# One pool for all eight PSUM banks, with a planner that follows each bank

## The chip, the cores and the metric

The kernel runs on one core of one Trainium2 chip. A core has five engines that run side by side, each through its own list of instructions: TensorE (PE in the profile) multiplies matrices, VectorE (DVE) and ScalarE (ACT) work elementwise and read TensorE's results, GpSimd (POOL) works elementwise on data in SBUF alone here, and SyncE (SP) issues nearly all transfers. TensorE writes its results into PSUM, which has eight banks. A bank holds 128 partitions x 512 float32 values, the largest result of one product here. Semaphores order the engines: an instruction that reuses a bank waits until the last reader of the bank has finished.

The metric is the time of one execution on the device in microseconds (us), as the median of several runs.

## The reference

Two parts follow each other. First comes attention by way of 32 learned points ("inducing"), for 4 batches of 12480 tokens with 128 channels:

```python
def mab(q, kv):
    s = scale * (q @ kv.transpose(0, 2, 1))
    s = s - s.max(-1, keepdims=True)
    a = np.exp(s)
    a /= a.sum(-1, keepdims=True) + 1e-09
    return a @ kv
h = mab(I, x)           # 32 points look at all tokens
return mab(x, h)        # all tokens look at the 32 results
```

Then comes a layer with a leaky relu, on all 49920 tokens, with 2048 hidden channels:

```python
h = x @ w_in
g = np.maximum(h, 0.0) + alpha * np.minimum(h, 0.0)
return g @ w_out
```

## The kernel before, in words

Tokens are taken in tiles of 128, and sixteen tiles make a superblock: six full ones per batch and a short rest. A token's attention output is a mixture of only 32 rows, so the first product of the layer is made from the 32 weights of each token: for each batch the kernel forms HW, the 32 results times w_in, and multiplies by the tokens' weights, which stand transposed in the tile `a` (a2 in the code). The leaky relu is split. The relu part goes through ACT or DVE, and then through a second product with W1, which is w_out scaled by one minus alpha. The linear part is one small product with a matrix HA per batch.

The main work is a chain of *visits*. A block is four tiles (512 tokens), and a block is visited four times, since each visit makes four of the sixteen groups of 128 hidden channels. In one visit TensorE makes four products into four banks (`visit`, L761). Each is read by one relu, on ACT (L774) or DVE (L776), which writes a tile `gt`. Behind these four products TensorE makes sixteen products from the `gt` tiles of the visit *before* (`second`, L787), which add up in the block's sum bank. At the first visit of every second block, `linear` (L814) adds the linear part into the sums of two blocks, and takes the second block's bank if it has none. When a block is complete, `finish` copies the sum to SBUF on ACT (L840) or DVE (L842; four early blocks at L833) and SP stores it (L847).

Between visits small pieces of work for the next superblock or batch are placed. For the next superblock: the scores (L597), their copy to SBUF (L655 on ACT, L657 on DVE), the maximum (L674, DVE), a subtraction (L679, GpSimd), the exponential (L641, ACT), a tree of sums (L665, GpSimd), a reciprocal (L702, DVE), the normalised weights in four copies (`rep`, L710, GpSimd) and a transposing transfer into `a` (L719, SP). For the next batch: loading x (L275), a cast (L290, GpSimd), a transposing transfer (`xT`, L313), scores (L336) and their reduction (L350, DVE), an exponential (L375, ACT), another transposing transfer (`e`, L406) and the sum over tokens (L430) with its addition (L446, DVE). SP works through loads, transposing transfers and stores in the order in which they were written down.

Two things fix the order. Which visit a small piece follows is written out by hand: `at(n, ...)` puts it behind visit n, with a list of its costs by engine. Which engine takes each relu and each copy, and whether a piece of elementwise work is done at once or late (between the second and third relu of the next visit, `run_waiting`), is chosen by the class `Plan` when the kernel is built: a search that keeps 64 states and steps through all visits with a small model of the engines' times. In that model a product of visit n has to wait for a relu that is fixed by a ring of six banks, and one number stands for when the separate bank is free.

The banks before: a pool of six, `hhps`, goes round for the four products of each visit and for everything in the opening. A second pool has two banks, bp0 and bp1. The blocks' sums alternate between them; after visit 8 a small product goes into the one that the current block doesn't use (`spare`).

Before the visits comes the opening (`order`, a list of steps by hand), in which the first batch's attention is made with casts and transposes on several engines and some empty products on TensorE ("W6") in between. One bank, `later`, keeps the scores of most of the first superblock until visit 1.

Of the kernel before, what the change touches and what calls it, by code (L numbers as in the profile page):

```python
# [21 lines left out]
P = 128  # L22
R = 4
ST = 16
# [6 lines left out]
def kernel(  # L31
# [55 lines left out]
    H = ST // 2  # L87
# [18 lines left out]

    hh_ps = ctx.enter_context(tc.tile_pool(name="hhps", bufs=6, space=bass.MemoryType.PSUM))
    b_ps = ctx.enter_context(tc.tile_pool(name="bps", bufs=1, space=bass.MemoryType.PSUM))

    ctx.enter_context(tc.manual_schedule())  # L110

    class Plan:
# [6 lines left out]
        FREE, MODE, SEM, ARRIVE = 56, 98, 62, 233  # L119
        WIDTH = 64  # L120

        def __init__(self):

            self.visits = []
            self.taken = None
            self.waiting = []

        def on_act(self):
# [14 lines left out]
        def step(self, state, n, relus, ways):  # L143


            pe, a, v, e1, e2, late, bank = state
            cols, last, linear, chains = self.visits[n]
            busy = {"a": a, "v": v}
            need = (e2[2], e2[3], e1[0], e1[1])
            hh = []  # L150
            for r in range(R):
                pe = max(pe, need[r] + self.SEM) + 4
                hh.append(pe + cols * 0.417 + self.ARRIVE)
            out = []
            for r in range(R):
                if r == 2:
                    for k, ns, ready, reads in late:
                        busy[k] = max(busy[k], ready) + ns
                        bank = busy[k] + 100 if reads else bank
                lat, per, over = self.RELU[relus[r]]  # L160
                out.append(max(busy[relus[r]], hh[r]) + lat + per * cols)
                busy[relus[r]] = out[r] - over
            pe += cols * 0.417
            if linear:
                pe = max(pe, bank + self.SEM) + linear
            pe += self.MODE
            for r in range(R):
                pe = max(pe, e1[r] + self.SEM) + last * self.FREE
            waits = []
            for chain, way in zip(chains, ways):  # L170
                ready, reads = 0, False
                for kind, ns in chain:
                    if kind == "!":
                        continue
                    if kind in "ps":
                        pe = max(pe, bank + self.SEM) if kind == "s" else pe
                        pe += ns
                        ready, reads = pe + self.ARRIVE, True
                        continue
                    k = way[0] if kind == "f" else kind  # L180
                    ns = self.COPY[k] if kind == "f" else ns
                    if way[-1:] == "l":
                        waits.append((k, ns, ready, reads))
                    else:
                        busy[k] = ready = max(busy[k], ready) + ns
                        bank = ready + 100 if reads else bank
                    reads = False
            return pe + self.MODE, busy["a"], busy["v"], tuple(out), e1, tuple(waits), bank

        def choose(self):  # L190
            zero = (0.0,) * R
            beam = [((0.0, 0.0, 0.0, zero, zero, (), 0.0), None)]
            relus = ["".join(w) for w in product("av", repeat=R) if 0 < w.count("a") < R]
            for n, (_, _, _, chains) in enumerate(self.visits):
                ways = []
                for chain in chains:
                    kinds = [k for k, _ in chain]
                    when = ["n", "l"] if len(ways) + 1 == len(chains) or "s" not in kinds else ["n"]
                    if "f" in kinds:
                        ways.append([e + w for e in "av" for w in when])  # L200
                    elif "!" in kinds or not {"a", "v"} & set(kinds):
                        ways.append([""])
                    else:
                        ways.append(when)
                found = {}
                for state, path in beam:
                    for way in product(*ways):
                        for relu in relus:
                            new = self.step(state, n, relu, way)
                            at = new[0] + 390  # L210
                            over = max(new[1] - at, 0) + max(new[2] - at, 0)
                            over += sum(w[1] for w in new[5]) * 0.3
                            score = new[0] + 0.3 * over
                            key = (*(int(x - new[0]) // 16 for x in new[1:3] + new[3]), new[5])
                            if key not in found or score < found[key][0]:
                                found[key] = (score, new, (path, relu + "".join(way)))
                best = sorted(found.values(), key=lambda f: f[0])[: self.WIDTH]
                beam = [(new, path) for _, new, path in best]
            path, taken = beam[0][1], []
            while path:  # L220
                path, these = path
                taken.append(these)
            self.taken = iter("".join(reversed(taken)))

    plan = Plan()

    def ring(shape, dtype=f32):
        return hh_ps.tile(shape, dtype, name="hh", tag="hh")

    def sums(k):  # L230

        return b_ps.tile([P, 512], f32, name="bp", tag=f"bp{k % 2}")

    spare = None

    def small(shape):

        if spare is None:
            return ring(shape)
        return b_ps.tile(shape, f32, name="hh", tag=f"bp{spare % 2}")  # L240

# [316 lines left out]
    def a_w_copy(st, act=True):  # L558
# [7 lines left out]
        plan.then(work)  # L566

    def a_lin(st):
# [210 lines left out]
    def second(blk, i, gts):  # L779
        nt = blk.nt  # L780
        if blk.acc is None:
            blk.acc = sums(blk.k)
        for r, gt in enumerate(gts):
# [15 lines left out]
    def linear(pair):  # L799


        for blk in pair:
            if blk.acc is None:
                blk.acc = sums(blk.k)
        products = [
# [106 lines left out]
    def warm(n):  # L912

        ps = sums(0)
        for _ in range(n):
            nc.tensor.matmul(ps[:, : 2 * P], blank[:, :P], blank[:], start=True, stop=True)  # L916
# [38 lines left out]
    w0 = rep0[:, :, 0, :]  # L955
    later = b_ps.tile([P, ST, M], f32, name="bp", tag="bp1")

# [197 lines left out]
    at(1, first_rest_less, H, H, cost=[("v", 780), ("!", 0)])  # L1155
    at(2, first_turn, cost=[("p", 350), ("f", 0)])
# [3 lines left out]
    at(6, linear_product, cost=[("p", 900), ("v", 210), ("!", 0)])  # L1160
    at(7, a_lin, st, cost=[("p", 260), ("v", 210)])
    blocks[0].later = True

# [23 lines left out]
    for b in range(B - 1):  # L1187
# [29 lines left out]
    for n, (blk, i) in enumerate(visits):  # L1217
        nt = visits[n - 1][0].nt * visits[n - 1][0].per if n else 0
        chains = [cost for _, _, cost in todo.get(n, ()) if cost]
        if i == 0 and n > NV:  # L1220
            copy = ("f", 0) if n > ST else ("v", 610)
            chains.insert(0, [("p", 0), copy])
            if n == 2 * NV:
                chains.insert(0, [("p", 0), copy])
        plan.visits.append((blk.nt * blk.per * P, nt, nt * Plan.FREE * (n in pairs), chains))
    plan.choose()

    prev = None
    for n, (blk, i) in enumerate(visits):
# [8 lines left out]
        if prev is not None:  # L1238
            second(*prev)
            spare = prev[0].k + 1 if n > 8 else None  # L1240
        prev = (blk, i, gts)
# [37 lines left out]
```

## Time and profile before

| | before |
|---|---|
| median of 3 runs | 601.63 us (601.0 to 601.75) |
| the profiled execution | 602.02 us |
| its span, first to last instruction | 599.8 us |
| visits begin at | 30.8 us |

The profile is of one execution, and its span is 2.2 us shorter than that execution's own time. In rows of groups stand the line, the engine, the operation, what is written and read with its shape, the count, then the busy time in us, the mean of one in ns, and the idle time of the engine just before with what ended it. In rows of the timeline stand the start in us, the time until the last of the row has ended, the engine and line, and the count; products overlap, so one row can begin before the row above it has ended. A wait of TensorE that is shorter than the products in flight doesn't show as idle time: it lengthens the row. In a row of windows restricted to a line stand the window, its length, the busy time of TensorE with the count of products, the busy time of the weight loads with their count, the granted clock, the share of the transfers and their GB/s.

### The profile page before, as it was taken

How to read it: one execution, taken by the hardware profiler on the slowest of the kernel's cores; microseconds unless marked ns; L12 is line 12 of the kernel's file. 1: busy time of each engine (PE TensorE's matmuls, PEld its weight loads, DVE VectorE, ACT ScalarE, POOL GpSimd, SP SyncE). 2: the span in 40 equal slices, each digit the busy share in tenths (PEclk: the TensorE clock that was granted, in tenths of full speed). 3: DMA queues.
4: the chain of work that ended last, by engine and by line, in shares of the span. 5: the costliest groups of instructions: out<-in, count | busy, mean ns of one | idle time of the engine just before them, and what ended most of it. 6: DMA issues, size and time to landing. Idle time of an engine off the chain costs nothing.

```text
span 599.8 us, 22813 instructions
## 1 busy us (share of the span) xinstructions
PE 590.2 (98%) x9501; PEld 442.6 (74%) x9501; DVE 518.9 (87%) x943; ACT 552.2 (92%) x1117; POOL 219.2 (37%) x261
## 2 busy tenths in 40 slices
PE   9899989999999999999999999999999999999997
PEld 6667767777777777777777777777777777777776
DVE  4778979888998899988898889988899899899986
ACT  6789989999999999999999999999999999999996
POOL 3595625303416436233136155233133133144010
PEclk9999999999999999999999999999999999999999
DMA  8946999443167996641357897931231341432311
GB/s 340 274 158 149 231 204 219 88 94 73 55 184 178 235 220 156 134 99 51 75 123 208 197 240 186 167 85 55 72 89 55 72 90 55 109 81 67 90 52 62
DMA packets 122344, 80.53 MB, mean 134 GB/s; under 512 B 103761, under 2 KB 106113, under 8 KB 119169
## 3 DMA queue, kind: packets, MB, share of 16 engines
q1 hardware_dynamic: 122016, 78.99, 54.7%
q8 instruction: 74, 1.21, 0.8%
q14 instruction: 30, 0.24, 0.1%
q10 hardware_dynamic: 224, 0.09, 0.1%
HBM read 28.07 MB, written 25.56 MB: 89 GB/s over the span
## 4 chain that ended last, share of the span: by engine, by line
PE 92%; DMA 4%; DVE 1%; issue 1%; SPq 1%; POOL 1%; ACT 0%; DVEq 0%; POOLq 0%
PE bp L787 63%; PE hh L761 22%; DMA a<-rep 2%; DMA xs<-in_x_dram 2%; PE bp L814 2%; PE hh L597 2%; PE hh L430 1%; PE hh L336 1%; POOL xn L309 1%; PE bp L916 0%; ACT gt L774 0%; DVE gt L776 0%; SPq L275 0%; PE hh L321 0%; PE hh L555 0%
## 5 line engine op out<-in xcount | busy, mean ns | idle before, releaser
L774 ACT ACTIVATE gt<-hh 128x512 bf16<-128x512 f32 x888 | 472.5, 608 | 30.1 <-PE hh L761 21.4
L776 DVE TENSOR_SCALAR gt<-hh 128x512 bf16<-128x512 f32 x672 | 435.1, 685 | 51.4 <-PE hh L761 40.4
L787 PE MATMUL bp<-W,gt 128*128 128x128 bf16 x6240 | 416.6, 220 | 0.2 <-DVE gt L776 0.2
L787 PEld LDWEIGHTS <-gt 128*128 128x128 bf16 x6240 | 349.4, 98 | 86.3 <-issue 79.5
L761 PE MATMUL hh<-a,HW 32*128 32x512 bf16 (+2 forms) x1664 | 158.9, 370 | 2.3 <-DMA a<-rep 1.7
L710 POOL TENSOR_TENSOR rep<-e,rc 128x2048 bf16<-128x2048 f32 (+1 forms) x24 | 84.5, 3521 | 19.6 <-DVE rc L702 19.1
L679 POOL TENSOR_TENSOR e<-e,smx 128x512 f32<-128x512 f32 (+1 forms) x24 | 24.6, 1026 | 169.6 <-DVE smx L674 169.6
L761 PEld LDWEIGHTS <-HW 32*128 32x128 bf16 x1664 | 40.7, 91 | 43.2 <-issue 7.7
L665 POOL TENSOR_TENSOR t<-e 128x256 f32<-128x256 f32 (+1 forms) x24 | 17.2, 718 | 132.5 <-ACT e L641 132.4
L840 ACT COPY ob<-bp 128x512 f32<-128x512 f32 (+1 forms) x62 | 36.6, 591 | 2.3 <-PE bp L787 1.4
L290 POOL CAST xn<-xs 128x2048 bf16<-128x2048 f32 x18 | 34.0, 1890 | 7.2 <-DMA xs<-in_x_dram 6.6
L665 POOL TENSOR_TENSOR t<-t 128x128 f32<-128x128 f32 (+3 forms) x100 | 30.4, 304 | 7.8
L350 DVE TENSOR_SCALAR_CACHE_REDUCE s<-hh 128x512 f32<-128x512 f32 (+2 forms) x29 | 18.1, 624 | 6.1 <-PE hh L336 5.8
L842 DVE COPY ob<-bp 128x512 f32<-128x512 f32 x32 | 21.8, 681 | 0.0
L814 PEld LDWEIGHTS <-a 32*128 32x128 bf16 x392 | 14.9, 93 | 6.6 <-issue 1.6
L814 PE MATMUL bp<-HA,a 32*128 32x128 bf16 x392 | 19.7, 214 | 0.1
L375 ACT ACTIVATE e1T<-s,rm 128x512 bf16<-128x512 f32 (+1 forms) x25 | 17.7, 707 | 0.3 <-DVE rm L359 0.3
L674 DVE TENSOR_REDUCE smx<-e 128x16 f32<-128x512 f32 (+1 forms) x24 | 15.9, 662 | 0.0
L641 ACT ACTIVATE e<-e 128x512 f32<-128x512 f32 (+1 forms) x24 | 14.8, 618 | 0.0
L916 PE MATMUL bp<-blank 128*128 128x256 bf16 x79 | 13.6, 314 | 1.2 <-DVE blank L862 1.2
L597 PE MATMUL hh<-hT,xT 128*128 128x32 bf16 x372 | 13.0, 176 | 0.1
L309 POOL CAST xn<-xs 128x512 bf16<-128x512 f32 (+1 forms) x12 | 8.8, 763 | 11.0 <-DMA xs<-in_x_dram 11.0
(110 smaller groups left out, 204.1 us busy)
## 6 DMA issues: line engine op xcount, KB each, us to landing
out_dram<-ob SPq DMA_DIRECT2D x97, 256.0 KB, 2.5
xs<-in_x_dram SPq DMA_DIRECT2D x23, 1024.0 KB, 6.0
xs<-in_x_dram SPq DMA_DIRECT2D x2, 512.0 KB, 8.5
w_in_f<-in_moe_w_in_dram SPq DMA_DIRECT2D x1, 1024.0 KB, 4.8
a<-rep SPq DMA_TRANSPOSE x25, 4.8
xT<-xn SPq DMA_TRANSPOSE x18, 6.0
e<-e1T SPq DMA_TRANSPOSE x18, 3.7
xs_left<-in_x_dram SPq DMA_DIRECT2D x4, 64.0 KB, 5.8
```

Of the source, the lines that this page charges most:

```text
L290: nc.gpsimd.tensor_copy(out=st.xn[s][:], in_=xs[:])
L597: nc.tensor.matmul(ps[w, t, :], st.xT[:, tile0[s] + t, w], hTs[b][:], start=True, stop=True)
L665: nc.gpsimd.tensor_tensor(out=t[:, :n], in0=src[:, :n, :w], in1=src[:, :n, w : 2 * w], op=ADD)
L679: nc.gpsimd.tensor_tensor(out=st.e2[s][:, :n], in0=st.e2[s][:, :n], in1=st.m2[s][:, :n].unsqueeze(2).broadcast_to([P, n, M]), op=SUB,)
L710: nc.gpsimd.tensor_tensor(out=rep[:, :n], in0=st.e2[s][:, :n].unsqueeze(2).broadcast_to([P, n, R, M]), in1=rc[:, :n].unsqueeze(2).unsqueez ...
L761: nc.tensor.matmul(hh[:, q * cols + w.start : q * cols + w.stop], HWs[b][rows, v * P : (v + 1) * P], a2[rows, t0 : t0 + nt, :].rearrange(" ...
L774: nc.scalar.activation(out=gt[:, :cols], in_=hh[:, :cols], func=RELU)
L776: nc.vector.tensor_relu(gt[:, :cols], hh[:, :cols])
L787: nc.tensor.matmul(blk.acc[:, t * C : (t + 1) * C], gt[:, (q * nt + t) * P : (q * nt + t + 1) * P], W1[:, k, :], start=(not blk.begun), st ...
L814: nc.tensor.matmul(blk.acc[w, t * C : (t + 1) * C], blk.a2[rows, blk.t0 + t, w], HAs[b][rows, :], start=(not blk.begun and t == 0), stop=F ...
L840: nc.scalar.copy(out=ob[:, :nt], in_=acc)
L842: nc.vector.tensor_copy(out=ob[:, :nt], in_=acc)
```

## The change

All eight banks are now in one pool with eight tags, k0 to k7, each with one buffer. The planner names the bank of every tile when the kernel is built. Its model keeps, for each bank, the time from which it is free; a bank that is in use is set to a time that never comes. For each of a visit's four products it takes the bank that is free earliest. For a small product, or a block's sum, it takes one among those that allow the earliest start. The model now also follows when a sum is begun, either at `linear` or before the second products, and when its copy lets it go. In the opening, where there is no plan yet, six banks go round as before; k6 takes the empty products and k7 the scores called `later`, and the plan has k7 from visit 1 on.

The list of choices is a little wider: a small product's elementwise work may be put late in more cases. The product HW and its copy are one step of the plan now instead of two. For the second batch, the loads of x for pieces 3 to 6 are issued three visits ahead of a mark instead of one, which is two visits sooner.

```diff
-    hh_ps = ctx.enter_context(tc.tile_pool(name="hhps", bufs=6, space=bass.MemoryType.PSUM))
-    b_ps = ctx.enter_context(tc.tile_pool(name="bps", bufs=1, space=bass.MemoryType.PSUM))
+    BANKS = 8
+    ps_pool = ctx.enter_context(tc.tile_pool(name="ps", bufs=1, space=bass.MemoryType.PSUM))
...
+        def bank(self):
+            if self.banks is not None:
+                return next(self.banks)
+            self.next += 1
+            return (self.next - 1) % (BANKS - 2)
...
-            need = (e2[2], e2[3], e1[0], e1[1])
-            hh = []
+            def take(pe):
+                k = min(range(BANKS), key=lambda k: max(free[k] + self.SEM, pe))
+                used.append(k)
+                pe = max(pe, free[k] + self.SEM)
+                free[k] = self.NEVER
+                return pe, k
+
+            hh, mine = [], []
             for r in range(R):
-                pe = max(pe, need[r] + self.SEM) + 4
+                k = min(range(BANKS), key=lambda k: free[k])
+                used.append(k)
+                mine.append(k)
+                pe = max(pe, free[k] + self.SEM) + 4
+                free[k] = self.NEVER
                 hh.append(pe + cols * 0.417 + self.ARRIVE)
...
                 out.append(max(busy[relus[r]], hh[r]) + lat + per * cols)
+                free[mine[r]] = out[r]
...
-            if linear:
-                pe = max(pe, bank + self.SEM) + linear
-            pe += self.MODE
+            for k in accs[0]:
+                if k not in held:
+                    pe, held[k] = take(pe)
+            pe += linear + self.MODE
+            for k in accs[1]:
+                if k not in held:
+                    pe, held[k] = take(pe)
...
     def ring(shape, dtype=f32):
-        return hh_ps.tile(shape, dtype, name="hh", tag="hh")
+        return ps_pool.tile(shape, dtype, name="hh", tag=f"k{plan.bank()}")
...
-            if b or p > 1:
-                at(m - 3 if b or p == 2 else m - 1, on, b + 1, a_load, pc)
+            if b or p > 1:
+                at(m - 3, on, b + 1, a_load, pc)
...
-        at(m + 12, on, b + 1, a_w, cost=[("s", 310)])
-        at(m + 12, on, b + 1, a_w_copy, cost=[("a", 487)])
+        at(m + 12, on, b + 1, a_w_both, cost=[("s", 310), ("a", 487)])
```

More of the change, by code (lines that the diff above doesn't have):

```diff
@@ L156, in step @@
                 if r == 2:
-                    for k, ns, ready, reads in late:
+                    for k, ns, ready, bank in late:
                         busy[k] = max(busy[k], ready) + ns
-                        bank = busy[k] + 100 if reads else bank
+                        if bank is not None:
+                            free[bank] = busy[k] + 100
                 lat, per, over = self.RELU[relus[r]]
                 out.append(max(busy[relus[r]], hh[r]) + lat + per * cols)
+                free[mine[r]] = out[r]
                 busy[relus[r]] = out[r] - over
             pe += cols * 0.417
-            if linear:
-                pe = max(pe, bank + self.SEM) + linear
-            pe += self.MODE
+            for k in accs[0]:
[5 more added lines that the diff above has]
+                    pe, held[k] = take(pe)
             for r in range(R):
@@ L170, in step @@
             for chain, way in zip(chains, ways):
-                ready, reads = 0, False
+                ready, bank = 0, None
                 for kind, ns in chain:
@@ L174, in step @@
                         continue
+                    if kind == "free":
+                        free[ns] = ready + 100
+                        continue
+                    if kind == "acc":
+                        ready, bank = pe + self.ARRIVE, held.pop(ns)
+                        continue
                     if kind in "ps":
-                        pe = max(pe, bank + self.SEM) if kind == "s" else pe
+                        if kind == "s":
+                            pe, bank = take(pe)
                         pe += ns
-                        ready, reads = pe + self.ARRIVE, True
+                        ready = pe + self.ARRIVE
                         continue
@@ L182, in step @@
                     if way[-1:] == "l":
-                        waits.append((k, ns, ready, reads))
+                        waits.append((k, ns, ready, bank))
                     else:
                         busy[k] = ready = max(busy[k], ready) + ns
-                        bank = ready + 100 if reads else bank
-                    reads = False
-            return pe + self.MODE, busy["a"], busy["v"], tuple(out), e1, tuple(waits), bank
+                        if bank is not None:
+                            free[bank] = ready + 100
+                    bank = None
+                if bank is not None:
+                    free[bank] = ready + 600
+            new = pe + self.MODE, busy["a"], busy["v"], tuple(out), tuple(free)
+            return (*new, tuple(held.items()), tuple(waits)), used
         def choose(self):
-            zero = (0.0,) * R
-            beam = [((0.0, 0.0, 0.0, zero, zero, (), 0.0), None)]
+            start = tuple(self.NEVER if k == BANKS - 1 else 0.0 for k in range(BANKS))
+            beam = [((0.0, 0.0, 0.0, (0.0,) * R, start, (), ()), None)]
             relus = ["".join(w) for w in product("av", repeat=R) if 0 < w.count("a") < R]
-            for n, (_, _, _, chains) in enumerate(self.visits):
+            for n, (*_, chains) in enumerate(self.visits):
                 ways = []
@@ L197, in choose @@
                     kinds = [k for k, _ in chain]
-                    when = ["n", "l"] if len(ways) + 1 == len(chains) or "s" not in kinds else ["n"]
                     if "f" in kinds:
-                        ways.append([e + w for e in "av" for w in when])
+                        ways.append([e + w for e in "av" for w in "nl"])
                     elif "!" in kinds or not {"a", "v"} & set(kinds):
@@ L208, in choose, with sums @@
                         for relu in relus:
-                            new = self.step(state, n, relu, way)
+                            new, used = self.step(state, n, relu, way)
                             at = new[0] + 390
                             over = max(new[1] - at, 0) + max(new[2] - at, 0)
-                            over += sum(w[1] for w in new[5]) * 0.3
+                            over += sum(w[1] for w in new[6]) * 0.3
                             score = new[0] + 0.3 * over
-                            key = (*(int(x - new[0]) // 16 for x in new[1:3] + new[3]), new[5])
+                            ends = sorted(max(x - new[0], -200) for x in new[4])
+                            key = (
+                                *(int(x - new[0]) // 16 for x in new[1:3] + new[3]),
+                                *(int(x) // 16 for x in ends if x < self.NEVER / 2),
+                                new[6],
+                            )
                             if key not in found or score < found[key][0]:
-                                found[key] = (score, new, (path, relu + "".join(way)))
+                                found[key] = (score, new, (path, relu + "".join(way), used))
                 best = sorted(found.values(), key=lambda f: f[0])[: self.WIDTH]
                 beam = [(new, path) for _, new, path in best]
-            path, taken = beam[0][1], []
+            path, taken, banks = beam[0][1], [], []
             while path:
-                path, these = path
+                path, these, used = path
                 taken.append(these)
+                banks.append(used)
             self.taken = iter("".join(reversed(taken)))
+            self.banks = iter([k for used in reversed(banks) for k in used])
     plan = Plan()
     def ring(shape, dtype=f32):
-        return hh_ps.tile(shape, dtype, name="hh", tag="hh")
[L230 to L240, printed above, removed]
+        return ps_pool.tile(shape, dtype, name="hh", tag=f"k{plan.bank()}")
+    small = ring
+    def sums():
+        return ps_pool.tile([P, 512], f32, name="bp", tag=f"k{plan.bank()}")
     class State:
@@ L803, in linear @@
             if blk.acc is None:
-                blk.acc = sums(blk.k)
+                blk.acc = sums()
         products = [
@@ L912, in warm @@
     def warm(n):
-        ps = sums(0)
+        ps = ps_pool.tile([P, 512], f32, name="bp", tag=f"k{BANKS - 2}")
         for _ in range(n):
@@ L955 @@
     w0 = rep0[:, :, 0, :]
-    later = b_ps.tile([P, ST, M], f32, name="bp", tag="bp1")
+    later = ps_pool.tile([P, ST, M], f32, name="bp", tag=f"k{BANKS - 1}")
     def first_products():
@@ L1217 @@
     for n, (blk, i) in enumerate(visits):
-        nt = visits[n - 1][0].nt * visits[n - 1][0].per if n else 0
+        before = visits[n - 1][0] if n else None
+        nt = before.nt * before.per if n else 0
         chains = [cost for _, _, cost in todo.get(n, ()) if cost]
@@ L1221 @@
             copy = ("f", 0) if n > ST else ("v", 610)
-            chains.insert(0, [("p", 0), copy])
+            chains.insert(0, [("acc", before.k), copy])
             if n == 2 * NV:
-                chains.insert(0, [("p", 0), copy])
-        plan.visits.append((blk.nt * blk.per * P, nt, nt * Plan.FREE * (n in pairs), chains))
+                chains.insert(0, [("acc", 0), copy])
+        both = [b.k for b in pairs.get(n, ())]
+        cost = nt * Plan.FREE if both else 0
+        plan.visits.append(
+            (blk.nt * blk.per * P, cost, (both, [before.k] if n else []), nt, chains)
+        )
     plan.choose()
```

24 lines of the change are left out of this document (15 added, 9 removed).

## The prediction

> **What bounds the kernel now.** I read the head of the page and the shares of the chain first, then the groups by line, then TensorE's timeline around the places where a product takes longer than its neighbours, and last the SP queue's timeline.
>
> ```profile
> span 599.8 us, 22813 instructions
> PE 590.2 (98%) x9501; PEld 442.6 (74%) x9501; DVE 518.9 (87%) x943; ACT 552.2 (92%) x1117; POOL 219.2 (37%) x261
> ...
> PEclk9999999999999999999999999999999999999999
> ...
> PE 92%; DMA 4%; DVE 1%; issue 1%; SPq 1%; POOL 1%; ACT 0%; DVEq 0%; POOLq 0%
> ...
> L774 ACT ACTIVATE gt<-hh 128x512 bf16<-128x512 f32 x888 | 472.5, 608 | 30.1 <-PE hh L761 21.4
> L776 DVE TENSOR_SCALAR gt<-hh 128x512 bf16<-128x512 f32 x672 | 435.1, 685 | 51.4 <-PE hh L761 40.4
> L787 PE MATMUL bp<-W,gt 128*128 128x128 bf16 x6240 | 416.6, 220 | 0.2 <-DVE gt L776 0.2
> ```
>
> TensorE (PE) is busy for 98% of the span, at the full clock in every slice, and carries 92% of the chain. ScalarE (ACT, 92%) and VectorE (DVE, 87%) come close behind, but they are paced by it. So a change that leaves TensorE's instructions alone can only win back what TensorE waits. How much that is shows in its timeline: a visit is four products of L761 and sixteen of L787.
>
> ```profile
> 117.83 0.40 PE L761 MATMUL hh<-a,HW 32*128 32x512 bf16 x4
> 118.16 1.07 PE L787 MATMUL bp<-W,gt 128*128 128x128 bf16 x16
> 119.16 0.50 PE L761 MATMUL hh<-a,HW 32*128 32x512 bf16 x4
> 119.59 1.07 PE L787 MATMUL bp<-W,gt 128*128 128x128 bf16 x16
> ...
> 267.89 0.61 PE L761 MATMUL hh<-a,HW 32*128 32x512 bf16 x4
> ```
>
> An undisturbed visit takes 119.16 - 117.83 = 1.33 us, and its four products 0.39 or 0.40. The visit at 119.16 has 0.50 and the one at 267.89 has 0.61: there the fourth product waited for its bank, which a relu had not yet let go. This wait hides inside busy time, so the list of waits does not carry it. The window rows restricted to L761 do:
>
> ```profile
> 60.00:110.00 50.00, 12.84 (x128) 3.30 (x124) 1.00 1.08 213
> 110.00:586.00 476.00, 134.64 (x1332) 33.77 (x1332) 1.00 0.49 116
> ```
>
> From 110 to 586 us there are 1332 / 4 = 333 groups of four; at 0.395 each they would take 131.5, and they took 134.64: 3.1 us of waits (1.4 to 4.8 with 0.40 or 0.39). From 60 to 110, 12.84 - 32 x 0.395 = 0.2. The whole of this long stretch offers 3.3 us. The start offers more per visit:
>
> ```profile
> 30.81 0.60 PE L761 MATMUL hh<-a,HW 32*128 32x512 bf16 x6
> 31.88 0.50 PE L761 MATMUL hh<-a,HW 32*128 32x512 bf16 x2 [0.47 <-ACT gt L774]
> ...
> 33.70 0.51 PE L761 MATMUL hh<-a,HW 32*128 32x512 bf16 x4
> ...
> 35.48 0.72 PE L761 MATMUL hh<-a,HW 32*128 32x512 bf16 x4
> ...
> 43.50 0.98 PE L761 MATMUL hh<-a,HW 32*128 32x512 bf16 x4
> ...
> 45.45 0.40 PE L761 MATMUL hh<-a,HW 32*128 32x512 bf16 x4
> 45.86 1.05 PE L787 MATMUL bp<-W,gt 128*128 128x128 bf16 x16
> ```
>
> The first eight products run from 30.81 to 32.38, 1.57 us. Its first row has six products in 0.60, so a second pair ends 0.1 to 0.2 behind the first four, and eight without a wait would take about 0.61 (an estimate from that row): 0.96 is waiting. Then 0.11, 0.32 and 0.58 over 0.40, and 0.41 from 45.45 to 45.86 where 0.33 is usual: 0.08. Together 2.05 us. Last, two of TensorE's waits are for a transfer:
>
> ```profile
> PE hh L761 <- DMA a<-rep: 1.7, 2, 1.3
> ```
>
> Sum of what can be won: 3.3 + 2.05 + 1.7, and 0.45 named below: 7.5 us of 602.
>
> **The change part by part.** The instruction lists of the two built programs show what a new plan made of it. TensorE's and GpSimd's orders are the same, instruction by instruction, so nothing is added or removed on TensorE and its 1.33 us visits stay. What differs is which bank each product writes, who empties it, and where SP's loads stand.
>
> *Banks.* Before, the four products of a visit went round six banks: the third waited for the first relu of the visit before, the fourth for the second. Two banks stood apart for block sums and small products. Now one sum is held most of the time and seven banks serve all else. In the lists the fourth product of 377 middle visits waits for a relu that is first on its engine in 327 cases and for ACT's second in 50 (331 and 46 before). The third has a relu of the visit before ahead of it in 124 visits instead of all 377. A first relu is ready about 0.33 + 0.61 to 0.69 after its visit begins, and the next visit begins at 1.33: 0.3 us to spare for an engine that is late. Of the 3.3 us I take 2.6; the bounds are 0 and 4.8 + 0.2.
>
> *The start.* At 43.50 the fourth product waited for ACT's third relu of the visit before; now it waits for the second, one step of ACT sooner:
>
> ```profile
> 42.48 3.08 ACT L774 ACTIVATE gt<-hh 128x512 bf16<-128x512 f32 x6 [0.70 <-PE hh L761]
> ```
>
> 3.08 / 6 = 0.51, so about 0.5 of that 0.58 goes. In the first visits a product gets its bank sooner, but L787 behind it reads the same relus' results and would wait instead, so of the other 1.47 I take 0.45. Together 0.95 (bounds 0 and 2.05).
>
> *Who does what.* ACT gives 40 relus to DVE and takes 10 copies of sums and 5 of scores from it; one turned block goes to DVE. From the rows above and L840 and L842,
>
> ```profile
> L840 ACT COPY ob<-bp 128x512 f32<-128x512 f32 (+1 forms) x62 | 36.6, 591 | 2.3 <-PE bp L787 1.4
> ...
> L842 DVE COPY ob<-bp 128x512 f32<-128x512 f32 x32 | 21.8, 681 | 0.0
> ```
>
> ACT becomes 552.2 - 40 x 0.608 + 15 x 0.591 - 0.6 = 536.1 and DVE 518.9 + 40 x 0.685 - 15 x 0.681 + 0.4 = 536.5. That is even, but DVE now has two relus in 314 middle visits, where it had two or three in 262. Two cost 2 x 0.61 by their distance when nothing waits (0.685 is one with its fill), under 1.33, with 0.11 left for its other work. The work is hidden as long as a backlog stays under the 0.3 above. I charge 0.3 us for new waits; the bounds are 0 and 63 visits (those with one relu only, that are left to absorb it) x 0.21 (the longer of the two waits shown, at 267.89) = 13.2.
>
> *Sums.* The second block of a pair takes its bank at L814. Two of these were held up:
>
> ```profile
> 61.53 0.66 PE L814 MATMUL bp<-HA,a 32*128 32x128 bf16 x8
> ...
> 74.06 0.62 PE L814 MATMUL bp<-HA,a 32*128 32x128 bf16 x8
> ...
> 136.47 0.43 PE L814 MATMUL bp<-HA,a 32*128 32x128 bf16 x8
> ```
>
> 0.66 and 0.62 against 0.43 make 0.42, and 0.39 is seen too: 0.45. Now this bank waits for a relu of the visit before in 47 of 48 pairs, first on its engine in all but one, so it is free by then. Gain 0.3 (bounds: a loss of 48 x 0.23 = 11 if all were as late as the one at 61.53, a gain of 0.45).
>
> *Loads.* For the second batch four loads of x move on SP. The first two get ahead of a store and a turn of xT, and of a store and a small turn of e; the others only ahead of a store.
>
> ```profile
> 57.12 2.52 SPq L313 DMA_TRANSPOSE xT<-xn  x1
> ...
> 67.33 0.57 SPq L275 DMA_DIRECT2D xs<-in_x_dram  x1
> 68.00 5.22 SPq L313 DMA_TRANSPOSE xT<-xn  x1
> 73.32 1.92 SPq L406 DMA_TRANSPOSE e<-e1T  x1
> ...
> 75.96 2.83 SPq L719 DMA_TRANSPOSE a<-rep  x1
> ...
> 79.46 0.45 SPq L275 DMA_DIRECT2D xs<-in_x_dram  x1
> 80.01 7.61 SPq L313 DMA_TRANSPOSE xT<-xn  x1
> ...
> 100.15 2.54 SPq L719 DMA_TRANSPOSE a<-rep  x1
> ```
>
> A turn directly behind a load holds SP for 5.22 and 7.61 us, one without for 2.52. The turn a<-rep at 75.96, for which TensorE waited 1.3 us, stood behind the one of 5.22. And GpSimd's casts, which start the rep, waited for these loads:
>
> ```profile
> 65.80 1.89 POOL L290 CAST xn<-xs 128x2048 bf16<-128x2048 f32 x1 [2.80 <-DMA xs<-in_x_dram]
> 73.40 1.89 POOL L290 CAST xn<-xs 128x2048 bf16<-128x2048 f32 x1 [2.14 <-DMA xs<-in_x_dram]
> ```
>
> A load two visits (2.7 us) sooner takes away the 2.80, and the turn loses its place right behind a load. So a<-rep comes some 2 us sooner: the 1.3 goes. The second wait, 0.4, hangs on the turn at 100.15, which moves less, while TensorE arrives earlier than before; I count no gain there. Gain 1.3 (bounds: 1.7, and a loss of 2.5, the difference between a turn behind a load and not, 5.22 - 2.52 = 2.7, if the moved load now holds up the turn at 57.12 and that comes out at TensorE). The stores behind loads wait 0.5 us longer; three output buffers cover them.
> The Trainium skill (DMA: Bandwidth & Descriptors, Queues, rings and completion order) has each DMA engine take the descriptors of a ring in order, with all of SP's transfers in one ring per engine. By that rule the load's bytes stand before the later turns wherever it is issued, and only gaps in the queue can swallow it; the 5.22 above agrees. The sum by it, with no gain here, is the second rival's.
>
> Sum: 0.95 + 2.6 + 1.3 + 0.3 - 0.3 = 4.85 us. The profiled run took 602.02 us (span 599.8), 0.4 above the median of 601.63, so 597.2 for it and 596.8 beside the median.
>
> **The rivals.**
> *DVE falls behind (slower).* With both of DVE's relus in sequence, the extra work (0.68 for a maximum, 0.69 for a score reduction) finds only 0.11 free per visit. If the 63 visits do not absorb it, each adds a wait between the 0.10 at 119.16 and the 0.21 at 267.89, say 0.15: 63 x 0.15 - 4.85 = +4.6 on 601.63, or 606.2. It decides from 4.85 / 0.15 = 32 such visits on. For it: those waits now follow DVE work. Against: busy times are even, 536 each.
> *The transfer waits stay.* The load only moves, another turn meets it, and 1.3 is not won: 598.1. For it: 5.22 and 7.61 behind loads. Against: the cast's 2.80.
> *The wait passes to L787.* Products get banks, but relus are no earlier, so L787 waits for them: half of 0.95 + 2.6 is lost, 598.6. Against: the last relu, second on DVE, is ready 0.33 + 0.69 + 0.61 = 1.63 after its visit begins and needed at 1.33 + 0.33 + 0.75 = 2.4.
> *No change.* The new plan trades one wait for another everywhere: 601.6.
>
> **How the numbers follow.** Forecast 0.48, transfer waits 0.18, L787 0.12, no change 0.08, DVE behind 0.14. About 0.2% (1.2 us) is what a measurement of this kernel can tell from nothing. Faster: 0.48 + 0.18 + 0.12 = 0.78; same 0.08; slower 0.14. The time is the forecast's, 596.8; its own range is 593.8 (1.1 more at the start, 0.4 more of the transfers, and 1.5 more of the long stretch, whose bound is 2.4 more) to 598.6 (half of the two bank terms). The range for all reaches up to 601.6 and leaves out the slower case.
>
> **What would show it.** Right: L761 from 110 to 586 us near 132 us, groups of 0.39 to 0.40; the group near 43.5 at about 0.5; no gap before L761 near 82; ACT and DVE both near 536. Wrong: groups of 0.5 to 0.6 in many visits, L787 runs over 1.07, gaps ended by a<-rep or DVE.

## The result, and the profile after

The changed kernel takes 597.21 us (median of 6 runs, 596.82 to 597.65) against 601.69 for the kernel before on the same occasions (6 runs, 601.0 to 602.04). The ratio is 0.9927, with a 95% interval from 0.9915 to 0.994: 0.7% faster. The prediction said 596.8.

First the head of the page, the shares of the chain, and the rows of the four main groups, of the changed kernel. Its lines have moved: L805 are the four products of a visit (L761 before), L831 the second products (L787), L858 the linear part (L814), L818 and L820 the relus on ACT and DVE (L774 and L776).

```profile
span 595.2 us, 23093 instructions
PE 586.6 (99%) x9501; PEld 442.6 (74%) x9501; DVE 531.3 (89%) x969; ACT 541.5 (91%) x1091; POOL 218.3 (37%) x261
...
PE 93%; DMA 4%; issue 1%; POOL 1%; SPq 0%; ACT 0%; DVE 0%; DVEq 0%; POOLq 0%
...
L818 ACT ACTIVATE gt<-hh 128x512 bf16<-128x512 f32 x848 | 453.4, 602 | 35.6 <-PE hh L805 27.8
L820 DVE TENSOR_SCALAR gt<-hh 128x512 bf16<-128x512 f32 x712 | 457.3, 684 | 29.1 <-PE hh L805 19.5
L831 PE MATMUL bp<-W,gt 128*128 128x128 bf16 x6240 | 416.1, 220 | 0.2 <-DVE gt L820 0.2
...
L805 PE MATMUL hh<-a,HW 32*128 32x512 bf16 (+2 forms) x1664 | 155.4, 370 | 1.0 <-ACT gt L818 0.5
```

Before, the products of a visit had this row:

```profile
L761 PE MATMUL hh<-a,HW 32*128 32x512 bf16 (+2 forms) x1664 | 158.9, 370 | 2.3 <-DMA a<-rep 1.7
```

The span is 4.6 us shorter (599.8 to 595.2), and TensorE has the same 9501 products in it. It is busy for 3.6 us less and idle for 1.0 us less. The smaller busy time is mostly that of the visit's products, 158.9 to 155.4: it is the waits for banks, which hide in busy rows. The windows restricted to the visit's products (window, length, busy time and count of products, then the weight loads, the granted clock, the share of the transfers, GB/s) say where:

```profile
60.00:110.00 50.00, 13.43 (x132) 3.33 (x132) 1.00 1.00 216
110.00:581.00 471.00, 131.29 (x1328) 33.37 (x1324) 1.00 0.50 117
```

A window counts a product that lies across its edge, and takes only the part of its busy time that lies inside. Two groups do so here, one of the changed kernel at 110 us and one of the kernel before at 60 us:

```profile
109.62 0.40 PE L805 MATMUL hh<-a,HW 32*128 32x512 bf16 x4
```

```profile
59.79 0.39 PE L761 MATMUL hh<-a,HW 32*128 32x512 bf16 x4
```

The first has 0.02 us in the long stretch, which therefore holds 331 whole groups and not 332. At 0.395 they would take 130.75, and they took 131.27: 0.5 us of waits is left of the 3.1. Between 60 and 110 us 33 groups took 13.45 with these 0.02, where 33 x 0.395 is 13.04, so 0.4 of waits. Before, 0.18 of the 12.84 belonged to the group that began at 59.79, and 31 whole groups took 12.66 instead of 12.25: 0.4 as well, and not the 0.2 that the prediction read. TensorE's timeline at the start of the visits and at two places where the linear part had to wait:

```profile
30.93 0.61 PE L805 MATMUL hh<-a,HW 32*128 32x512 bf16 x7
32.03 0.37 PE L805 MATMUL hh<-a,HW 32*128 32x512 bf16 x1 [0.49 <-ACT gt L818]
...
33.73 0.45 PE L805 MATMUL hh<-a,HW 32*128 32x512 bf16 x4
...
35.45 0.39 PE L805 MATMUL hh<-a,HW 32*128 32x512 bf16 x4
...
43.15 0.49 PE L805 MATMUL hh<-a,HW 32*128 32x512 bf16 x4
43.61 0.40 PE L858 MATMUL bp<-HA,a 32*128 32x128 bf16 x8
...
60.90 0.38 PE L858 MATMUL bp<-HA,a 32*128 32x128 bf16 x8
...
74.10 0.40 PE L805 MATMUL hh<-a,HW 32*128 32x512 bf16 x4
74.33 0.39 PE L858 MATMUL bp<-HA,a 32*128 32x128 bf16 x8
```

The first eight products run from 30.93 to 32.40, 1.47 us where it was 1.57. The groups of 0.51, 0.72 and 0.98 have become 0.45, 0.39 and 0.49, and the late start of L787 near 45.5 (0.08) is gone. Of the 0.49 that the third of them lost, TensorE won only 0.16, because the linear part behind it did not wait for the group's end. Before, it began 0.62 after the group (43.50 to 44.12):

```profile
44.12 0.40 PE L814 MATMUL bp<-HA,a 32*128 32x128 bf16 x8
```

Now it begins 0.46 after the group (43.15 to 43.61), where 0.23 is usual (74.10 to 74.33): 0.09 of that is the group's own wait, and 0.14 is new. The two linear parts of 0.66 and 0.62 take 0.38 and 0.39. TensorE's waits for transfers, from the list of waits:

```profile
PE hh L376 <- DMA xT<-xn: 1.1, 1, 1.1
...
PE hh L805 <- DMA a<-rep: 0.5, 1, 0.5
```

The waits for a<-rep fell from 1.7 to 0.5, and one for the turn of xT came in their place.

One wait of the kernel before, which the prediction did not count, is gone too. A score product (L336) needed the bank that `spare` also gave to the sum over tokens ahead of it (L430), and DVE's addition (L446) still read it. From that sum to the visit's products it was 1.04 us:

```profile
78.26 0.28 PE L430 MATMUL hh<-xn_left,e 128*32 128x128 bf16 x2
78.97 0.40 PE L336 MATMUL hh<-xT,IT 128*32 128x512 bf16 x4 [0.43 <-DVE hs L446]
79.30 0.39 PE L761 MATMUL hh<-a,HW 32*128 32x512 bf16 x4
```

In the changed kernel it is 0.43, so 0.6 is won:

```profile
78.30 0.23 PE L470 MATMUL hh<-xn_left,e 128*32 128x128 bf16 x1
...
78.73 0.39 PE L805 MATMUL hh<-a,HW 32*128 32x512 bf16 x4
```

Put together, in us:

| term | forecast | shown by the rows |
|---|---|---|
| start of the visits | 0.95 | 0.10 + 0.06 + 0.33 + 0.16 + 0.08 = 0.7 |
| banks in the rest (60 us on) | 2.6 | 3.1 + 0.4 - 0.5 - 0.4 = 2.6 |
| sums' banks at the linear part | 0.3 | 0.28 + 0.23 = 0.5 |
| new waits by DVE's load | -0.3 | none found |
| transfers | 1.3 | 1.7 - 0.5 - 1.1 = 0.1 |
| a score product's bank near 79 us | not in the sum | 0.6 |
| first visit begins later (30.81, 30.93) | 0 | -0.1 |
| sum | 4.85 | 4.4, of a span that is 4.6 shorter |

The same products in the same order allow a check, since the start of one product can be compared in the two traces. The changed kernel is 0.1 behind at the first visit, 0.6 ahead near 46 us (L787 at 45.86, L831 at 45.27), and 4.6 ahead at the end. So the start gave 0.7, as the table has it.

The table explains the spans of two executions. Of the 4.5 us between the medians, 0.4 lie outside the span: an execution takes 2.2 to 2.4 us beyond its span in every run with the old split of relus, and 1.75 to 1.9 in every run with the new one. No row shows what that is.

### The profile page after: what moved, and what is told of

Same layout as the page of the kernel before. It is cut to its first block, busy times and chain, and to the rows that moved or that the text cites. A ratio compares the mean times of both kernels' runs of the same rounds, so it can differ in the third digit from the quotient of the medians.

```text
span 595.2 us, 23093 instructions
## 1 busy us (share of the span) xinstructions
PE 586.6 (99%) x9501; PEld 442.6 (74%) x9501; DVE 531.3 (89%) x969; ACT 541.5 (91%) x1091; POOL 218.3 (37%) x261
## 4 chain that ended last, share of the span: by engine, by line
PE 93%; DMA 4%; issue 1%; POOL 1%; SPq 0%; ACT 0%; DVE 0%; DVEq 0%; POOLq 0%
PE bp L831 64%; PE hh L805 21%; DMA xs<-in_x_dram 2%; PE bp L858 2%; PE hh L641 2%; DMA xT<-xn 2%; PE hh L470 1%; PE hh L376 1%; DMA a<-rep 1%; POOL xn L349 1%; PE bp L960 0%; ACT gt L818 0%; SPq L315 0%; PE hh L361 0%; PE hh L595 0%
## 5 line engine op out<-in xcount | busy, mean ns | idle before, releaser
L818 ACT ACTIVATE gt<-hh 128x512 bf16<-128x512 f32 x848 | 453.4, 602 | 35.6 <-PE hh L805 27.8
L820 DVE TENSOR_SCALAR gt<-hh 128x512 bf16<-128x512 f32 x712 | 457.3, 684 | 29.1 <-PE hh L805 19.5
L831 PE MATMUL bp<-W,gt 128*128 128x128 bf16 x6240 | 416.1, 220 | 0.2 <-DVE gt L820 0.2
L831 PEld LDWEIGHTS <-gt 128*128 128x128 bf16 x6240 | 349.3, 98 | 83.8 <-issue 76.4
L805 PE MATMUL hh<-a,HW 32*128 32x512 bf16 (+2 forms) x1664 | 155.4, 370 | 1.0 <-ACT gt L818 0.5
L805 PEld LDWEIGHTS <-HW 32*128 32x128 bf16 x1664 | 40.2, 91 | 41.1 <-issue 5.0
L884 ACT COPY ob<-bp 128x512 f32<-128x512 f32 x72 | 42.3, 587 | 4.6 <-PE bp L831 1.4
L886 DVE COPY ob<-bp 128x512 f32<-128x512 f32 x22 | 15.2, 691 | 6.5 <-PE bp L831 6.3
L858 PEld LDWEIGHTS <-a 32*128 32x128 bf16 x392 | 15.0, 93 | 5.9 <-issue 0.3
L858 PE MATMUL bp<-HA,a 32*128 32x128 bf16 x392 | 19.1, 214 | 0.0
L699 ACT COPY e<-hh 128x512 f32<-128x512 f32 (+1 forms) x24 | 14.2, 594 | 0.1
```

Source lines behind the costliest of these rows:

```text
L805: nc.tensor.matmul(hh[:, q * cols + w.start : q * cols + w.stop], HWs[b][rows, v * P : (v + 1) * P], a2[rows, t0 : t0 + nt, :].rearrange(" ...
L818: nc.scalar.activation(out=gt[:, :cols], in_=hh[:, :cols], func=RELU)
L820: nc.vector.tensor_relu(gt[:, :cols], hh[:, :cols])
L831: nc.tensor.matmul(blk.acc[:, t * C : (t + 1) * C], gt[:, (q * nt + t) * P : (q * nt + t + 1) * P], W1[:, k, :], start=(not blk.begun), st ...
L858: nc.tensor.matmul(blk.acc[w, t * C : (t + 1) * C], blk.a2[rows, blk.t0 + t, w], HAs[b][rows, :], start=(not blk.begun and t == 0), stop=F ...
L884: nc.scalar.copy(out=ob[:, :nt], in_=acc)
```

## The experiments

Below, theory and rivals stand as they were written down before each run. In all kernels TensorE and GpSimd have the same instructions in the same order as in both kernels here; only banks, the engines and moments of relus, copies and small elementwise pieces, and the place of loads differ. Unless a row is shown, the medians of several runs are compared with the kernel before on the same chip (601.75 to 601.83).

**The loads put back.**

```diff
-                at(m - 3, on, b + 1, a_load, pc)
+                at(m - 3 if b or p == 2 else m - 1, on, b + 1, a_load, pc)
```

> The changed kernel with the four loads of x back at their old visits; banks, relus and copies as in the changed kernel. Theory (the gain is the banks' and the new plan's, the loads bring nothing): the wait for the turn xT near 66 us (1.1 us) goes, and the waits for a<-rep near 82 and 106 us (1.3 and 0.5) come back; the time stays within 0.5 us of the changed kernel's 597.2. Rival (the sooner loads bring the 1.3 us that was forecast): 598.5.

597.35 us (597.26 to 597.40 in three runs, and 598.98 in the profiled one, of which the last section tells more); ratio to before 0.9933 (0.9916 to 0.995). So the loads bring nothing in the changed kernel. The wait for xT is gone, and that for a<-rep is back, in the profiled execution as one of 2.0 us:

```profile
PE hh L805 <- DMA a<-rep: 2.0, 1, 2.0
```

**The loads alone.** The kernel before with the same line in the other direction.

> The kernel before with only the four loads two visits sooner; banks, relus and copies as before. Theory (loads bring nothing): a wait of about 1 us for the turn xT near 67 us, less wait for a<-rep, and 601.7 within 0.5 us. Rival (loads bring 1.3 us): 600.4.

601.91 us, ratio 1.0002 (0.9992 to 1.0011): nothing, as the theory says. TensorE's list of waits has 1.0 for the turn of xT at L336, and none for a<-rep:

```profile
PE hh L336 <- DMA xT<-xn: 1.0, 1, 1.0
```

The two together settle the share: the whole gain comes from banks and plan.

**The new split of relus with the old banks.** The plan is made as in the changed kernel, and its relus, copies and late pieces are kept; the banks are given out as before.

```diff
     plan.choose()
+    plan.banks = None          # ring(): k0 to k5 in turn
...
+    def sums(k):
+        return ps_pool.tile([P, 512], f32, name="bp", tag=f"k{BANKS - 2 + k % 2}")
+    def small(shape):
+        if spare is None:
+            return ring(shape)
+        return ps_pool.tile(shape, f32, name="hh", tag=f"k{BANKS - 2 + spare % 2}")
```

> The changed kernel's relus, copies and loads, instruction by instruction, but with the banks given out as before (a ring of six, and two apart for sums and small products). Theory (free banks are what makes the new split of relus possible): in the ring the fourth product waits for the second relu, and in the new split that is second on ACT or DVE in most visits, ready 0.33 + 0.60 + 0.48 = 1.41 after its visit begins where 1.33 is wanted; 0.08 in some 300 visits, up to 24 us, and so slower than before: 605 to 625. Rival (the new split of relus brings the gain by itself, its engines being evenly loaded): 597 to 599.

668.35 us, ratio 1.1108 (1.1089 to 1.1126). The direction was right and the size was not. The products of a visit carry most of it, 50 of the 67 us, by their row of the groups; a stretch of TensorE's timeline stands below it, with DVE's beside it:

```profile
L811 PE MATMUL hh<-a,HW 32*128 32x512 bf16 (+2 forms) x1664 | 208.8, 369 | 7.5 <-DVE gt L826 0.8
```

```profile
92.53 0.40 PE L811 MATMUL hh<-a,HW 32*128 32x512 bf16 x4
92.86 1.07 PE L837 MATMUL bp<-W,gt 128*128 128x128 bf16 x16
93.86 0.88 PE L811 MATMUL hh<-a,HW 32*128 32x512 bf16 x4
```

```profile
93.03 1.29 DVE L826 TENSOR_SCALAR gt<-hh 128x512 bf16<-128x512 f32 x2 [0.42 <-PE hh L811]
```

In this kernel's instruction list the fourth product waits for the relu that is second on its engine in 356 of 377 middle visits: 267 on ACT and 89 on DVE. In the kernel before it was ACT's second in 46, by the prediction's count. The expectation had priced ACT's. The row at 93.86 shows DVE's: two relus begin at 93.03 and the second is done at 94.32, while the products began at 93.86, so the group takes 0.88, or 0.48 more than usual. Sorted by the plan's list, from the eleventh visit on, the 290 groups behind two relus of ACT are together 23 us over their usual length, 0.08 each as expected. The 90 behind two of DVE are 35 us over it, and those are what the expectation left out. Another 10 us are waits of small products for a bank that ACT's copy of a sum (L890) still read, mostly in this row of TensorE's list of waits:

```profile
PE hh L647 <- ACT ob L890: 8.3, 13, 0.7
```

The new split by itself is no gain; it is one that only free banks can bear.

**Free banks with the old split.** The plan may only take the choices that the kernel before had, visit by visit (a list of 390 short words); it still places the banks.

```diff
                         for relu in relus:
+                            if relu + "".join(way) != OLD[n]:
+                                continue
                             new, used = self.step(state, n, relu, way)
```

> The changed kernel's free banks and loads, but with each relu, copy and late piece on the engine and at the place that the kernel before had. Theory (banks are the cause): most waits for a bank go even so, 598 to 599.5. Rival (the split of relus is the cause): 601.5, with as many groups of 0.5 to 0.6 us as before.

598.78 us, ratio 0.9953 (0.9938 to 0.9968). Free banks alone bring 3.0 of the 4.5 us; the new split adds about 1.5 on top. The window of its visits' products (L834):

```profile
110.00:580.00 470.00, 131.32 (x1320) 33.45 (x1320) 1.00 0.49 117
```

330 groups at 0.395 are 130.35, so 1.0 us of waits is left here, between the 3.1 of before and the 0.5 of the changed kernel. That is some 0.4 of the 1.5, and another 0.4 lies outside the span. For the rest no single row stands out. The run puts late pieces back along with the relus, so it does not tell the new split from the wider list of choices.

**Seven banks.** The planner is not told that k7 is free after the opening.

```diff
-    at(1, first_rest_less, H, H, cost=[("v", 780), ("free", BANKS - 1), ("!", 0)])
+    at(1, first_rest_less, H, H, cost=[("v", 780), ("!", 0)])
```

> The changed kernel, but the planner never gets the eighth bank in the visits (k7 stays out after the opening), so it plans with seven. Theory (the eighth bank gives the room): with one sum held, six are left for all else, and part of the gain goes: 598.5 to 601. Rival (following each bank's release is enough, the number does not matter): 597.2 within 0.5.

608.48 us, ratio 1.011 (1.0094 to 1.0127): slower than before, while the theory (598.5 to 601) and the rival both had it faster. The products' row:

```profile
L805 PE MATMUL hh<-a,HW 32*128 32x512 bf16 (+2 forms) x1664 | 164.8, 370 | 0.5 <-ACT gt L818 0.5
```

They are busy for 9.4 us more than with eight. The plan was made for seven, with new choices of its own, and still left these waits; whether a better plan for seven exists was not tried. Following the banks is not enough: with this planner the eighth is worth 11 us.

**Two loads early.** In the idle time of SP, behind visits 6 and 9.

```diff
-                at(m - 3, on, b + 1, a_load, pc)
+                at({3: 6, 4: 9}.get(p, m - 3) if not b else m - 3, on, b + 1, a_load, pc)
```

> The changed kernel with the loads of pieces 3 and 4 of the second batch issued behind visits 6 and 9, when SP stands idle (39 to 47 us), instead of 12 and 20. Theory (a turn of xT behind a load takes SP 5.5 us instead of 2.5, and its wait of 1.1 us took the place of the a<-rep wait): the turn near 57 us takes about 2.5 us, its landing is in time, the second cast of GpSimd no longer waits 3.5 us, the a<-rep wait shrinks: 595.4 to 596.3. Rival (the bytes only meet another turn): 597.2, with a wait for a<-rep or xT elsewhere.

597.73 us, ratio 0.9933 (0.9918 to 0.9947): no gain over the changed kernel. SP's timeline shows that the second of these loads did not get into the idle time. It stood behind a turn that waited and two stores, and so came right before the next turn:

```profile
47.65 1.85 SPq L763 DMA_TRANSPOSE a<-rep  x1
49.60 1.50 SPq L891 DMA_DIRECT2D out_dram<-ob  x2
51.16 0.45 SPq L315 DMA_DIRECT2D xs<-in_x_dram  x1
51.70 6.51 SPq L353 DMA_TRANSPOSE xT<-xn  x1
```

```profile
PE hh L376 <- DMA xT<-xn: 1.8, 1, 1.8
```

SP's idle time was itself a wait for the next transfer of its list, and what is written down behind that transfer waits too. The turn took SP 6.51 us, and TensorE waited 1.8 for it, an earlier turn than in the changed kernel. At this point the runs fit both readings: the place matters, or the bytes do. The next two runs tell them apart.

**One load early, the other left or moved behind a turn.** The first keeps only `{3: 6}` of the edit above; the second has `{3: 6, 4: 14}`, where 14 is right behind the visit whose turn is issued near 57 us.

> The changed kernel with the load of piece 3 alone put behind visit 6, when SP is idle; the others as in the changed kernel. Theory (the turn xT near 57 us was held up by this one load right ahead of it, and the turn near 51 us was held up in the run before only because the load of piece 4 came behind it in time): neither turn is held up, the wait for xT goes, the wait of 0.5 us for a<-rep near 80 us stays or grows up to 0.7: 595.8 to 596.5. Rival (the transfers between 45 and 105 us are limited by their bytes, so a wait of 1 us or more turns up somewhere): 597.0 to 597.7.

> As the run with one load early, and the load of piece 4 behind visit 14, where SP has just issued the turn near 57 us, instead of behind visit 20. Theory: GpSimd's second cast no longer waits 3.5 us for it, the turn a<-rep comes sooner and its wait of 0.5 us goes too: 595.3 to 596.0. Rival (bytes): 597.0 to 597.7.

595.47 us (595.04 to 595.92), ratio 0.9888 (0.9873 to 0.9903), and 595.78 us (595.5 to 595.85), ratio 0.9894 (0.988 to 0.9908). Both beat the changed kernel, and neither has a wait of TensorE for a turn left. SP's timeline of the first, with no load ahead of the two turns:

```profile
51.64 3.07 SPq L353 DMA_TRANSPOSE xT<-xn  x1
54.80 1.61 SPq L353 DMA_TRANSPOSE xT<-xn_left  x1
56.50 0.53 SPq L891 DMA_DIRECT2D out_dram<-ob  x1
57.12 2.16 SPq L353 DMA_TRANSPOSE xT<-xn  x1
```

The bytes are the same, so place decides. The gain, 1.7 us in the medians, is the 1.1 + 0.5 that TensorE waited. The second edit adds nothing, as there was no wait left for it. The expected stay of the a<-rep wait in the first was wrong: it went too, and the time came out below the expected 595.8 to 596.5.

**The same loads in the kernel before.** `{3: 6, 4: 14}` with the old banks and split.

> The kernel before with the loads of pieces 3 and 4 behind visits 6 and 14; banks, relus and copies as before. Theory (with the loads out of the way the two a<-rep waits, 1.3 and 0.5 us, go at least in part, whatever the banks): 600.0 to 600.8. Rival: 601.7.

600.57 us, ratio 0.9975 (0.9965 to 0.9985), 1.3 us less, as the theory says. TensorE's list of waits has none for a<-rep or xT. So the transfers' waits and the banks' are separate, and their gains add: 1.3 here, 1.7 in the changed kernel.

## Why the prediction was right, and where it was not

*The bound* held: with TensorE's instructions unchanged, only its waits could be won, 7.5 us by the prediction's count, and 4.6 were.

*The bank terms* held: 0.7 for 0.95 at the start, 2.6 for 2.6 in the rest, 0.5 for 0.3 at the linear part. The start was sized wrongly. At 43.50 the prediction counted the group's whole 0.58 as lost and 0.5 as won. The linear part behind it had begun only 0.39 later than usual, and 0.16 of that was won. The step about L787 did not happen as told: the eighth product still waited for a relu (0.49 at 32.03), and L831 behind it did not begin to wait (0.30 later, where 0.33 is usual). The other places of the start gave 0.57 where 0.45 was taken. And the bound left out the score product's bank, which was worth 0.6.

*DVE's load* was charged 0.3, and none of it was found. The two longest groups that are left behind the start are these:

```profile
62.21 0.60 PE L805 MATMUL hh<-a,HW 32*128 32x512 bf16 x4
...
69.27 0.52 PE L805 MATMUL hh<-a,HW 32*128 32x512 bf16 x4
```

By the plan's list of banks, the fourth product of both waits for a relu of ACT. The busy times were sized wrongly: 536.1 and 536.5 were forecast, and 541.5 (ACT) and 531.3 (DVE) measured. The prediction took 40 relus at their full 0.608 and 0.685, but a relu's fill overlaps the end of the one before. The groups' own busy time fell by 472.5 - 453.4 = 19.1 and rose by 457.3 - 435.1 = 22.2, 0.48 and 0.56 for each.

*The loads* are the step that failed: "the 1.3 goes". The a<-rep waits did shrink by 1.2. But the moved load stood ahead of the turn at 57, and what the prediction had kept for its lower bound happened, at less than half of the cost that it had there:

```profile
56.12 0.57 SPq L315 DMA_DIRECT2D xs<-in_x_dram  x1
56.78 0.38 SPq L891 DMA_DIRECT2D out_dram<-ob  x1
57.26 5.50 SPq L353 DMA_TRANSPOSE xT<-xn  x1
```

That turn took 5.50 us instead of 2.52, its landing came 8.98 us after its issue by the chain, and the score product waited 1.1. The term was worth 0.1, as the second rival had it. The GpSimd cast for which a wait of 2.80 was to go did stop waiting; the next one then waited longer:

```profile
71.54 1.89 POOL L330 CAST xn<-xs 128x2048 bf16<-128x2048 f32 x1 [3.49 <-DMA xs<-in_x_dram]
```

That the time came out within 0.4 us of the forecast is in part luck. The loads brought 1.2 less than forecast and the start 0.25 less. The score product's bank gave 0.6 that was in no term, the linear part 0.2 more, and the 0.3 charged for DVE stayed away.

*The rivals.* DVE did not fall behind. The wait did not pass to L787: its busy time fell by 0.5. The runs show how near the other side was, however: the same split on the old banks costs 67 us, and the same planner with seven banks 7.

## What to carry to other kernels

Where one engine is busy all the time, measure its hidden waits first, as the excess of a repeated group over its usual length. That gave the size of the three bank terms to within 0.3 us each, though no list of waits showed them. What such an excess costs shows at the start of the work behind it: the group of 0.58 over its usual length held TensorE up by 0.39. A split of work over engines and the banks that it needs belong to one plan: neither can be judged alone, since the new split with its late pieces was worth 1.5 us with free banks and cost 67 without. And a large load is not free when it is early: look at what stands directly behind it in its queue, and put it where that is nothing urgent.

## What the runs showed of the hardware that was not expected

How long a transposing transfer held SP depended on the load ahead of it. The turn near 57 us held it for 2.16 with none (the run with one load early) and for 5.50 with one of 1 MB shortly before (the changed kernel). The turn near 51 us held it for 3.07 in that run and for 6.51 behind a load (the run with two loads early). The Trainium skill (DMA: Bandwidth & Descriptors, Queues, rings and completion order) has descriptors consumed in ring order on each engine. These rows agree with it, and so does the run with one load early: issued into a gap of the queue, behind visit 6, the same load cost TensorE nothing. No run here shows what holds SP itself.

In the profiled execution of the run with the loads put back, TensorE was granted half of its clock for some 3.4 us, and that execution took 1.6 us longer than the other three. It came right behind the wait of 2.0 us for a<-rep, which ended at 81.52. The windows restricted to the second products (L831) show the granted clock, the third figure from the end of a row:

```profile
82.00:84.00 2.00, 1.65 (x16) 1.38 (x14) 0.50 1.00 395
84.00:86.00 2.00, 1.65 (x16) 1.48 (x16) 0.65 1.29 198
86.00:88.00 2.00, 1.70 (x28) 1.53 (x29) 1.00 1.11 173
```

TensorE's shorter waits for transfers in the other profiles, of up to 1.8 us (the run with two loads early), had no such drop behind them. One execution does not show whether the longer wait brought it about.
